# Small VectorE operations issued in a row, sixteen steps of attention read out in float32, and another block order in the last step

## The chip, the cores and the metric

The kernel runs on one core of a Trainium2 chip. Its engines are TensorE (PE; PEld is its weight load), VectorE (DVE), ScalarE (ACT), GpSimd (POOL) and SyncE (SP, which here issues nearly all DMAs). The metric is device time in microseconds (us): the median of three runs, 929.9 us (929.48 to 930.02). Times in rows count from the start of the profiled span.

## The reference

Attention with a memory, then two feed-forward layers ("MoE"), each with two matrix products:

```python
# B, H, S, D = 4, 8, 576, 64; 2304 tokens, d_model 512, d_ff 2048
scores = where(causal, -1e9, q @ k.T / sqrt(D)); a = softmax(scores); local = a @ v
q_p = where(q > 0, q, exp(q) - 1) + 1
mem_out = (q_p @ M_prev) / (q_p @ z_prev + 1e-6)
x = g * mem_out + (1 - g) * local                 # g = sigmoid(beta) per head
h = x @ moe_w_in;  x = (h * sigmoid(h)) @ moe_w_out
h = x @ moe2_w_in; return (h * tanh(softplus(h))) @ moe2_w_out
```

## The kernel before

**Attention** works on pairs of heads. A visit is one pair and either its first two blocks of 128 queries or its last three; the 16 visits of the first kind come first. A step is one block of queries of a visit (`STEPS`), in three stages. `stage_a`: scores (PE), their maximum (DVE, L613), the exponential (ACT), and P, the unnormalized weights, brought into transposed form. `stage_b`, three steps later: P times V and the memory product (PE), then, at a visit's last step, a chain of DVE operations: the denominators (add, reciprocal, multiply: 8 columns each) and the scaled result (512 columns). `stage_c`: a transpose and the way to `xs0` or DRAM.

P is transposed in two ways. In the first `TURNED` = 8 steps PE transposes the float32 P, ACT copies it out of PSUM, and P times V is one float32 matmul per block of keys. In later steps ACT and DVE split P into two float16 parts (`copy`, `stt`), a DMA transposes them, and each block of keys takes three float16 matmuls; V is then split too (`prep_v`: a DVE maximum at L538, a PE sum, three small DVE operations, ACT, DVE).

**Weights** of the first MoE come in 16 units of 1 MB, 0 to 7 for `w_in` and 8 to 15 for `w_out`. Each is rebuilt from 64-bit words (`single`: two ACT operations, one DVE), and PE multiplies it with itself (a gram matrix; `banks<-w 128x128` in the rows) for a bound of its size. `part_scale` turns the bound into a scale by a chain of small DVE operations (`largest`, `inverse`), for `w_in` in two halves and for `w_out` once; then ACT and DVE split each unit into two float16 parts (`weight_split`; `w<-w,wsc` in the rows).

**The MoE** runs in 9 chunks of 256 tokens, 8 units of width each. `chunk_x` loads and scales a chunk's inputs (`xh<-xs,xsc`); `gemm1` (`banks<-xh,w`), `hidden` and `gemm2` (`banks<-g,w`) follow. The second MoE is alike, with 7 products in place of 8 (`p` in `gemm2`); `flush2` combines the 7 blocks on ACT and DVE and stores them.

**The order** of all this is set by `Plan`: every operation is recorded with its reads, writes and priority, and `issue` walks through modelled time, giving each engine the ready operation with the lowest priority number. The engines then run their lists in that order, and an instruction whose input is late holds all behind it. When PE is idle in the plan between 18 and 75 us, it gets filler matmuls (`L474`).

Of the kernel before, what the change touches and what calls it, by code (L numbers as in the profile page):

```python
# [9 lines left out]
F32 = mybir.dt.float32  # L10
# [37 lines left out]
TURNED = 8  # L48
FILL_FROM, FILL_TO, FILL_PART, FILL_NS = 18e3, 75e3, 0.6, 28
PARTS = 2  # L50
# [12 lines left out]
class Plan:  # L63
# [6 lines left out]
    def __init__(self):  # L70
        self.ops, self.seen, self.shared, self.fill = [], {}, set(), None
# [13 lines left out]
    def add(self, prio, choices, writes, reads, tail=0, edge=(0, 0, (False, False), (False, False)), shared=False):  # L85


        k, deps = len(self.ops), set()
        for regs, w in ((reads, False), (writes, True)):
            for r in [y for x in regs for y in self.regions(x)]:  # L90
                log = self.seen.setdefault(r[0], [])
                keep = []
                for e in log:
                    _, a0, a1, b0, b1, op, ew = e
                    hit = a0 < r[2] and r[1] < a1 and b0 < r[4] and r[3] < b1
                    if hit and (w or ew) and op != k:
# [100 lines left out]
def attn_moe_moe2_kernel(ctx: ExitStack, tc: tile.TileContext, kq, vm, beta, w1, w2, out):  # L197
# [13 lines left out]
    plan = Plan()  # L211
# [285 lines left out]
    def load_vm(v, prio):  # L497
        p, _, nk = VISITS[v]
        n = nk * 2 * (D + 1)
        if 2 * v < TURNED:  # L500
            t = phs[v // 2 * 2].rearrange("p n c -> p (n c)").bitcast(F32)[:, 260 * (v % 2):260 * (v % 2) + n]
        else:
            t = rvr()[:, 0:n]
        rm[v] = rmr()
        rv[v] = t.rearrange("p (n e d) -> p n e d", n=nk, e=2)
        dma(prio, t, vm[p, :, 130:130 + n], reads=[])
        dma(prio, rm[v], vm[p, :, 0:130], reads=[])
# [22 lines left out]
    def prep_v(v, prio):  # L530
# [10 lines left out]
        mm(prio, [(total, ones, top, True, True)])  # L541
        ts(prio, inv[:, 0:2], total.to_broadcast([128, 2]), 2.0**-14, ALU.mult, 1e-30, ALU.max)
        ts(prio, inv[:, 0:2].bitcast(U32), inv[:, 0:2].bitcast(U32), 0x7F800000, ALU.bitwise_and)
        other(prio, "DVE", 80, lambda: nc.vector.reciprocal(out=scale, in_=inv[:, 0:1]), [scale], [inv])
        plan.add(prio, [c_act(v1[:, :, :, 0:D], x, AF.Copy, scale), (*c_ts(v1[:, :, :, 0:D], x, scale, ALU.mult), VC)],
# [97 lines left out]
    def stage_b(n, prio):  # L643
# [37 lines left out]
        each = lambda y: y.unsqueeze(1).to_broadcast([128, m, 4])  # L681
        tt(prio, den, g[:, :, :, D], each(eps[:, 4 * (n < TURNED):4 * (n < TURNED) + 4]), ALU.add)
        other(prio, "DVE", 90, lambda: nc.vector.reciprocal(out=den, in_=den), [den], [den])
        tt(prio, den, den, each(gvv), ALU.mult)
        tt(prio, t4, g[:, :, :, 0:D], den.unsqueeze(3).to_broadcast([128, m, 4, D]), ALU.mult)
        tt(prio, x, t4[:, :, 0:2], t4[:, :, 2:4], ALU.add, ("POOL", "DVE"))
# [29 lines left out]
    def largest(prio, s, top, spot, root=0.0):  # L716


        d, m = diagr(), mxr()[:, 1:2]
        if cols(top) == 128:  # L720
            stt(prio, d, top, 1e-30, ident, ALU.max, ALU.mult)
        else:
            ts(prio, d, ident, top, ALU.mult, 1e-30, ALU.max)
        if spot is None:
            o = banks[:, 512 * 6:512 * 8].rearrange("p (b c) -> p b c", b=2)[:, :, 388:452]
            mm(prio, [(o[:, i], onesf, d[:, 64 * i:64 * i + 64], True, True) for i in range(2)])
            reduce(prio, m, o, ALU.max, mybir.AxisListType.XY)
# [15 lines left out]
    def part_scale(g, prio):  # L743

        c, w = cvec[0], wsc[0]
        if g < PARTS:
            largest(prio, w[:, g:g + 1], gram[0], bank[0], WMAX[0][0] / 4)
            inverse(prio, c[:, 4 + g:5 + g], w[:, g:g + 1])
            ts(prio, c[:, 4 + g:5 + g], c[:, 4 + g:5 + g], 0.5, ALU.mult)
            return  # L750
# [6 lines left out]
        ts(prio, c[:, 2:3], t, 0.5, ALU.mult)  # L757

    def weight_scale(l, k, prio, spot):
# [10 lines left out]
        else:  # L770
            tt(prio, c[:, 2:3], c[:, 2:3], p, ALU.mult)

# [80 lines left out]
    def chunk_x(l, c, prio, spot):  # L853
# [7 lines left out]
        top = top[:, 0:1]  # L861
        reduce(prio, top, r, ALU.max, mybir.AxisListType.XY, True)
        tt(prio, t16, top, top, ALU.mult)
        mm(prio, [(spot, ones, t16, True, True)])
        ts(prio, p, spot, 1e-36, ALU.max)
        inverse(prio, s, p)
        ts(prio, s.bitcast(U32), s.bitcast(U32), 1, ALU.logical_shift_right, 0x7F800000, ALU.bitwise_and)
        ts(prio, s, s, 2.0**64 * XNORM, ALU.mult)
        if l == 0:
# [11 lines left out]
        inverse(prio, p, s)  # L881
# [68 lines left out]
    def gemm2(l, j, g, yo, prio):  # L950
        if l == 1:
            for p in (2, 1, 4, 6, 7, 5, 3):
# [91 lines left out]
    def weights_of(k, gate=()):  # L1044

        nonlocal n_att
        for u in range(NU // 2 * k, NU // 2 * (k + 1)):
# [5 lines left out]
            if k == 0 and j == NU // 2 // PARTS - 1:  # L1053
                part_scale(g, w_prio(u))
                for w in range(u - j, u + 1):
                    weight_split(w, w_prio(u))
        if k == 1:
            part_scale(PARTS, w_prio(u))
# [55 lines left out]
    for i, (l, c, j) in enumerate(steps):  # L1114
# [7 lines left out]
        gemm2(l, j, g_of.pop(i), y_of[l, c], 1e6 + i)  # L1122
# [55 lines left out]
```

## Time and profile before

| | |
|---|---|
| median of three runs | 929.9 us |
| the profiled execution, its span | 929.32 us, 927.3 us |
| busy PE, DVE, ACT, POOL | 897.8, 706.9, 594.7, 438.5 us |
| granted TensorE clock, mean of the span | 0.997 |

Busy time is the union of an engine's instructions, so a wait between two of them is not in it. In a timeline row the first number is the start, the second the time from the first start to the last end of what is merged in the row ("x8"), and in brackets stands the idle time before it with what ended it.

### The profile page before, as it was taken

Reading aid. Unit: us, or ns where it says so; the run is one execution under the profiler, and the core shown is the slowest. Engines: PE = TensorE matmul, PEld = TensorE weight load, DVE = VectorE, ACT = ScalarE, POOL = GpSimd, SP = SyncE. Lnnn points to the kernel's source line nnn. Section 1 sums busy time; section 2 is a strip of 40 time slices with the busy share of each in tenths; the row PEclk is TensorE's granted clock in tenths of the full one; section 3 lists DMA queues with packets and bytes.
Section 4 is the critical chain, followed back from the end, with each engine's and each line's share of the span. In section 5 each row is a group of like instructions: output and inputs, shape, how many; then the busy total and the mean of one; then the engine's idle time right before and its main releaser. Section 6 shows DMA issues by size and latency. Waiting matters only on the chain.

```text
span 927.3 us, 26260 instructions
## 1 busy us (share of the span) xinstructions
PE 897.8 (97%) x10830; PEld 808.4 (87%) x10830; DVE 706.9 (76%) x1512; ACT 594.7 (64%) x1032; POOL 438.5 (47%) x653
## 2 busy tenths in 40 slices
PE   6889799999999999999999999999999999999997
PEld 5778688888888888888988889999999999999996
DVE  4798977887988688878567465578787887887775
ACT  6799878788687787866465445445455545644553
POOL 3104223645555444564477466363554644635443
PEclk9999999999999999999999999999999999999999
DMA  8799589898999898985434353301010010010010
GB/s 272 260 226 290 161 185 312 204 272 215 240 249 239 241 226 208 231 179 102 115 116 126 136 172 126 104 25 47 19 31 25 25 47 25 24 47 17 10 24 23
DMA packets 148759, 129.77 MB, mean 140 GB/s; under 512 B 105376, under 2 KB 132512, under 8 KB 144544
## 3 DMA queue, kind: packets, MB, share of 16 engines
q1 hardware_dynamic: 148496, 128.10, 52.0%
q8 instruction: 84, 1.38, 0.6%
q14 instruction: 35, 0.29, 0.1%
q10 hardware_dynamic: 144, 0.00, 0.0%
HBM read 77.75 MB, written 25.69 MB: 112 GB/s over the span
## 4 chain that ended last, share of the span: by engine, by line
PE 91%; ACT 4%; DVE 3%; issue 1%; SPq 0%; DMA 0%; DVEq 0%; ACTq 0%
PE banks L427 89%; ACT arena L359 2%; PE banks L435 1%; DVE w L367 1%; ACT w L779 1%; DVE arena L373 1%; ACT w L359 1%; DVE arena L613 0%; PE banks L474 0%; SPq L441 0%; ACT ws L359 0%; DMA arena<-vm 0%; DVE arena L367 0%; DVE ws L367 0%; ACT ga L359 0%
## 5 line engine op out<-in xcount | busy, mean ns | idle before, releaser
L427 PEld LDWEIGHTS <-w 128*128 128x128 f16 (+1 forms) x3584 | 342.0, 98 | 41.1 <-issue 2.1
L427 PE MATMUL banks<-arena 128*128 128x128 f16 (+5 forms) x4728 | 287.2, 221 | 5.8 <-ACT arena L359 4.6
L427 PEld LDWEIGHTS <-arena 128*128 128x128 f16 x4392 | 226.0, 98 | 7.5 <-issue 4.4
L427 PE MATMUL banks<-xh,w 128*128 128x256 f16 x1728 | 206.6, 273 | 0.0
L427 PE MATMUL banks<-g,w 128*128 128x256 f16 x1728 | 205.5, 273 | 0.0
L373 POOL TENSOR_TENSOR arena<-arena 128x4 f32<-128x4 f32 (+3 forms) x147 | 96.8, 663 | 178.6 <-DVE arena L373 78.8
L427 PE MATMUL banks<-w,g 128*128 128x256 f16 x1512 | 178.9, 273 | 0.0
L427 PEld LDWEIGHTS <-g 128*128 128x128 f16 x1512 | 144.4, 98 | 15.2
L373 POOL TENSOR_TENSOR g<-ga,g 128x512 f16<-128x512 f32 x72 | 96.3, 1340 | 69.3 <-ACT g L359 68.9
L359 ACT ACTIVATE arena<-arena 128x256 f32<-128x256 f32 (+7 forms) x169 | 98.9, 606 | 32.7 <-PE banks L427 30.5
L373 POOL TENSOR_TENSOR w<-w 128x128 f32<-128x128 f32 x138 | 78.3, 590 | 87.1 <-ACT w L359 85.5
L367 DVE SCALAR_TENSOR_TENSOR arena<-arena 128x640 f16<-128x640 f32 (+6 forms) x132 | 105.5, 805 | 12.6 <-ACT arena L359 9.6
L373 POOL TENSOR_TENSOR xh<-xh 128x128 f32<-128x128 f32 x138 | 68.2, 516 | 53.7 <-ACT xh L359 51.9
L359 ACT ACTIVATE arena<-banks,arena 128x128 f32<-128x128 f32 (+4 forms) x144 | 74.5, 551 | 21.0 <-DVE arena L613 16.2
L359 ACT ACTIVATE ga<-banks,xsc 128x512 f32<-128x512 f32 x72 | 49.4, 686 | 48.6 <-PE banks L427 46.5
L367 DVE SCALAR_TENSOR_TENSOR g<-w,xsc,g 128x384 f16<-128x384 f32 (+1 forms) x72 | 52.1, 725 | 29.2 <-ACT g L359 29.2
L613 DVE TENSOR_REDUCE arena<-banks 128x2 f32<-128x256 f32 (+3 forms) x80 | 63.6, 802 | 13.8 <-PE banks L427 11.8
L367 DVE SCALAR_TENSOR_TENSOR ga<-ga,banks 128x512 f32<-128x512 f32 x72 | 48.8, 680 | 31.9 <-ACT ga L359 31.6
L359 ACT ACTIVATE w<-banks 128x128 f32<-128x128 f32 x72 | 19.7, 273 | 62.4 <-PE banks L427 62.3
L373 DVE TENSOR_TENSOR arena<-banks,arena 128x8 f32<-128x8 f32 (+1 forms) x96 | 36.3, 378 | 29.4 <-PE banks L427 14.7
L367 DVE SCALAR_TENSOR_TENSOR g<-xh,xsc,g 128x384 f16<-128x384 f32 (+1 forms) x72 | 53.5, 746 | 5.9 <-ACT g L359 4.5
L359 ACT ACTIVATE g<-w,xsc 128x384 f16<-128x384 f32 (+1 forms) x72 | 47.4, 661 | 10.6 <-POOL w L373 10.0
(128 smaller groups left out, 1142.8 us busy)
## 6 DMA issues: line engine op xcount, KB each, us to landing
ws<-w SPq DMA_DIRECT2D x22, 1024.0 KB, 7.0
arena<-kq SPq DMA_DIRECT2D x16, 576.0 KB, 4.8
w<-w SPq DMA_DIRECT2D x8, 1024.0 KB, 5.6
wd<-w SPq DMA_DIRECT2D x16, 512.0 KB, 3.7
arena<-vm SPq DMA_DIRECT2D x16, 325.0 KB, 4.2
yd<-w SPq DMA_DIRECT2D x36, 128.0 KB, 2.7
ws<-wd SPq DMA_DIRECT2D x9, 512.0 KB, 4.3
xs<-yd SPq DMA_DIRECT2D x9, 512.0 KB, 3.7
```

The source lines that it names most:

```text
L359: return ("ACT", ns, lambda: nc.scalar.activation(out=out, in_=in_, func=func, scale=scale, bias=bias))
L367: return ("DVE", 1.04 * cols(out) + 160 - over[0], lambda: nc.vector.scalar_tensor_tensor(out=out, in0=in0, scalar=s, in1=in1, op0=op0, op ...
L373: return (e, ns, lambda: eng.tensor_tensor(out=out, in0=in0, in1=in1, op=op))
L427: nc.tensor.matmul(out=o, lhsT=l, rhs=r, start=a, stop=z)
L435: plan.add(prio, [("PE", 109, lambda: nc.tensor.transpose(o, x, ident))], [o], [x, ident], edge=(107, 109, (False, False), (False, False)))
L613: other(prio, "DVE", 1.04 * cols(both) + 70, lambda: nc.vector.tensor_reduce(out=m1, in_=both, axis=AX, op=ALU.max, negate=True), [m1], [b ...
L779: plan.add(prio, [("ACT", 0.833 * 1024 + 115, lambda: nc.scalar.activation(out=w, in_=high.bitcast(F32), func=AF.Prelu, scale=2.0**-112, a ...
```

## The change

Four things change. (1) `Plan` can record several small DVE operations as one (`begin`, `close`): they are then issued one behind the other, with nothing between. This is done for the denominators with the scaled result, the three small operations of `prep_v`, the chains of `part_scale` and `weight_scale`, and two in `chunk_x`, whose `inverse(p, s)` moves up. (2) `TURNED` is 16, so visits 4 to 7 take the float32 way too; all eight visits keep V in `phs`, three to a buffer. (3) `part_scale` gets priority -3e5 (before: `w_prio`, about -2e5 for `w_in` and 35 for `w_out`). (4) The last `gemm2` takes its blocks in the order 1, 7, 2, 6, 4, 5, 3.

```diff
-TURNED = 8
+TURNED = 16
...
+    def begin(self):
+        self.run = []
+
+    def close(self, prio):
+        run, self.run = self.run, None
+        cs = [next(c for c in r[0] if c[0] == "DVE") for r in run]
+        def go():
+            for c in cs:
+                c[2]()
+        return self.add(prio, [("DVE", sum(c[1] for c in cs), go)], [x for r in run for x in r[1]],
+                        [x for r in run for x in r[2]], shared=any(r[3] for r in run))
...
         if 2 * v < TURNED:
-            t = phs[v // 2 * 2].rearrange("p n c -> p (n c)").bitcast(F32)[:, 260 * (v % 2):260 * (v % 2) + n]
+            t = phs[v // 3].rearrange("p n c -> p (n c)").bitcast(F32)[:, 260 * (v % 3):260 * (v % 3) + n]
...
+        plan.begin()
         tt(prio, den, g[:, :, :, D], each(eps[:, 4 * (n < TURNED):4 * (n < TURNED) + 4]), ALU.add)
         other(prio, "DVE", 90, lambda: nc.vector.reciprocal(out=den, in_=den), [den], [den])
         tt(prio, den, den, each(gvv), ALU.mult)
         tt(prio, t4, g[:, :, :, 0:D], den.unsqueeze(3).to_broadcast([128, m, 4, D]), ALU.mult)
+        plan.close(prio)
...
+        plan.begin()
         ts(prio, p, spot, 1e-36, ALU.max)
         inverse(prio, s, p)
         ts(prio, s.bitcast(U32), s.bitcast(U32), 1, ALU.logical_shift_right, 0x7F800000, ALU.bitwise_and)
         ts(prio, s, s, 2.0**64 * XNORM, ALU.mult)
+        inverse(prio, p, s)
+        plan.close(prio)
...
-            for p in (2, 1, 4, 6, 7, 5, 3):
+            for p in (1, 7, 2, 6, 4, 5, 3) if ended else (2, 1, 4, 6, 7, 5, 3):
...
-            part_scale(PARTS, w_prio(u))
+            part_scale(PARTS, -3e5)
```

The instructions move as follows. First VectorE, where the scale of `w_out` is made; `mx_84` is the bound, `wsc_0_89` the scales, `cvec_0_91` the constants made of them, and `arena_95` belongs to attention. Before:

```order
L376 TENSOR_REDUCE mx_84<-banks 128x1
L367 SCALAR_TENSOR_TENSOR arena_95<-arena_95 128x256
L741 RECIPROCAL wsc_0_89<-mx_84 128x1
L367 SCALAR_TENSOR_TENSOR arena_95<-arena_95 128x256
L364 TENSOR_SCALAR wsc_0_89<-wsc_0_89 128x1
L367 SCALAR_TENSOR_TENSOR arena_95<-arena_95 128x512
L364 TENSOR_SCALAR wsc_0_89<-wsc_0_89 128x1
L373 TENSOR_TENSOR arena_95<-banks,arena_95 128x8
L364 TENSOR_SCALAR arena_95<-arena_95 128x2
L613 TENSOR_REDUCE arena_95<-banks 128x2
L373 TENSOR_TENSOR cvec_0_91<-cvec_0_91,wsc_0_89 128x1
L683 RECIPROCAL arena_95<-arena_95 128x8
```

With the change:

```order
L394 TENSOR_REDUCE mx_84<-banks 128x1
L765 RECIPROCAL wsc_0_89<-mx_84 128x1
L382 TENSOR_SCALAR wsc_0_89<-wsc_0_89 128x1 x2
L394 TENSOR_REDUCE cvec_0_91<-wsc_0_89 128x1
L391 TENSOR_TENSOR cvec_0_91<-cvec_0_91,wsc_0_89 128x1
L385 SCALAR_TENSOR_TENSOR wsc_0_89<-cvec_0_91 128x2
L765 RECIPROCAL cvec_0_91<-cvec_0_91 128x1
L382 TENSOR_SCALAR cvec_0_91<-cvec_0_91 128x1
L385 SCALAR_TENSOR_TENSOR ga_78<-ga_78,banks 128x512
L391 TENSOR_TENSOR xsc_86<-cvec_0_91,xsc_86 128x1
L385 SCALAR_TENSOR_TENSOR arena_95<-arena_95 128x256
L385 SCALAR_TENSOR_TENSOR w_72<-w_72,wsc_0_89 128x1024
```

Before, eight operations of the chain took up 20 places of the list, with twelve of attention between them (the last is `L364` on `cvec_0_91`, eight rows further down; a ninth came earlier). Now the nine stand together (`x2` is two of them).

Next, VectorE at the start of the program. L538 (L556 after the change) is the maximum of V in `prep_v`, L613 (L633) that of the scores. Before:

```order
L538 TENSOR_REDUCE arena_95<-arena_95 128x1
L613 TENSOR_REDUCE arena_95<-banks 128x2 x2
L538 TENSOR_REDUCE arena_95<-arena_95 128x1
L613 TENSOR_REDUCE arena_95<-banks 128x2 x2
L364 TENSOR_SCALAR arena_95<-banks 128x2
L364 TENSOR_SCALAR arena_95<-arena_95 128x2
L544 RECIPROCAL arena_95<-arena_95 128x1
L364 TENSOR_SCALAR arena_95<-arena_95 128x4x64
```

With the change:

```order
L633 TENSOR_REDUCE arena_95<-banks 128x2 x4
L556 TENSOR_REDUCE arena_95<-arena_95 128x1 x2
L391 TENSOR_TENSOR arena_95<-banks,arena_95 128x8
L704 RECIPROCAL arena_95<-arena_95 128x8
L391 TENSOR_TENSOR arena_95<-arena_95 128x8
L391 TENSOR_TENSOR arena_95<-banks,arena_95 128x512
L385 SCALAR_TENSOR_TENSOR w_72<-w_72,ws_76 128x1024
L633 TENSOR_REDUCE arena_95<-banks 128x2 x2
```

The maximum of V, of the first visit that takes the float16 way, stood ahead of the scores' and now stands behind them, and the first chain of denominators has moved ahead of the first rebuilt unit (`w_72<-w_72,ws_76`).

Last, SP at the start of the program: `vm` is V and the memory matrices, `kq` keys and queries, `w` the weight units. Before:

```order
L441 DMA arena_95<-vm 128x260 x3
L441 DMA arena_95<-vm 128x130
L441 DMA arena_95<-vm 128x260
L441 DMA ws_76<-w 128x2048
L441 DMA ws_77<-w 128x2048
L441 DMA g_75<-w 128x2048
L441 DMA arena_95<-kq 128x2x256 x2
L441 DMA arena_95<-vm 128x260
```

With the change:

```order
L459 DMA arena_95<-vm 128x260 x3
L459 DMA arena_95<-vm 128x130
L459 DMA arena_95<-vm 128x260 x5
L459 DMA arena_95<-kq 128x2x256
L459 DMA ws_76<-w 128x2048
L459 DMA ws_77<-w 128x2048
L459 DMA g_75<-w 128x2048
L459 DMA arena_95<-kq 128x2x256
```

Four more loads of V and one of keys and queries now stand ahead of the first three weight units.

## Rows read from the trace of the kernel before

**Rows 1.** Busy time by stretch; the bracket counts instructions, PEclk is the granted clock
```profile
0.00:61.50 61.50, 47.40 (x671) 40.58 (x672) 40.97 (x100) 45.78 (x81) 13.78 (x37) 1.00 0.79 261
61.50:94.90 33.40, 31.83 (x355) 27.54 (x354) 29.79 (x54) 31.92 (x60) 13.01 (x10) 1.00 1.06 264
94.90:103.60 8.70, 3.68 (x40) 2.98 (x40) 8.21 (x28) 5.74 (x12) 1.72 (x3) 0.91 0.74 203
103.60:150.00 46.40, 44.62 (x466) 37.85 (x465) 39.55 (x99) 37.12 (x79) 11.46 (x15) 0.98 0.79 191
150.00:450.00 300.00, 298.95 (x3464) 259.55 (x3462) 245.22 (x475) 230.79 (x393) 147.63 (x203) 1.00 0.91 219
450.00:920.60 470.60, 470.60 (x5837) 439.56 (x5835) 340.26 (x754) 242.91 (x411) 250.85 (x387) 1.00 0.19 60
```
Columns: stretch and length, then PE, PEld, DVE, ACT, POOL, PEclk, DMA share, GB/s.

**Rows 2.** Timeline of PE, 94 to 105 us
```profile
94.26 0.62 PE L427 MATMUL banks<-w 128*128 128x128 bf16 x8
...
96.06 0.49 PE L427 MATMUL banks<-diag,onesf 128*128 128x128 f32 x2 [1.18 <-DVE diag L367]
...
102.26 0.16 PE L427 MATMUL banks<-arena,ones 128*128 128x1 bf16 x1 [3.86 <-DVE arena L538]
...
103.58 1.49 PE L427 MATMUL banks<-g,w 128*128 128x256 f16 x6
```

**Rows 3.** Timeline of DVE in the chain of the scale of w_out
```profile
96.60 0.28 DVE L376 TENSOR_REDUCE mx<-banks 128x1 f32<-128x128 f32 x1
...
97.13 0.15 DVE L741 RECIPROCAL wsc<-mx 128x1 f32<-128x1 f32 x1
97.20 0.40 DVE L367 SCALAR_TENSOR_TENSOR arena<-arena 128x256 f32<-128x256 f32 x1
...
100.20 0.15 DVE L367 SCALAR_TENSOR_TENSOR wsc<-cvec 128x2 f32<-128x2 f32 x1
```

**Rows 4.** Timeline of ACT, the first split units of w_out
```profile
101.29 2.18 ACT L359 ACTIVATE w<-w,wsc 128x1024 f16<-128x1024 f32 x2
```

**Rows 5.** Timeline of DVE, two dependent small operations with nothing between
```profile
10.84 0.17 DVE L364 TENSOR_SCALAR arena<-arena 128x2 uint32<-128x2 uint32 x1
11.05 0.16 DVE L544 RECIPROCAL arena<-arena 128x1 f32<-128x1 f32 x1
```

**Rows 6.** Timeline of PE: P times V in float32, transposes, P times V in float16
```profile
33.45 1.38 PE L427 MATMUL banks<-arena 128*128 128x65 f32 x10 [0.47 <-ACT xs L359]
34.66 0.82 PE L435 MATMUL banks<-ident,arena 128*128 128x128 f32 x6
...
71.52 0.83 PE L427 MATMUL banks<-arena 128*128 128x65 f16 x14
```

**Rows 7.** ACT by form, 58.9 to 101.3 us (busy us, mean ns of one)
```profile
L359 ACT ACTIVATE arena<-arena 128x256 f16<-128x256 f32 x7 | 3.0, 449 | 0.0
...
L359 ACT ACTIVATE arena<-arena 128x512 f16<-128x512 f32 x4 | 2.5, 625 | 0.0
```

**Rows 8.** DVE by form, 58.9 to 101.3 us
```profile
L367 DVE SCALAR_TENSOR_TENSOR arena<-arena 128x256 f16<-128x256 f32 x6 | 4.1, 686 | 0.0
...
L367 DVE SCALAR_TENSOR_TENSOR arena<-arena 128x512 f16<-128x512 f32 x4 | 3.6, 890 | 0.1
```

**Rows 9.** Timeline of SP, DVE and ACT at the program's start
```profile
2.13 4.39 SPq L441 DMA_DIRECT2D arena<-vm  x9
...
7.95 0.42 DVE L538 TENSOR_REDUCE arena<-arena 128x1 bf16<-128x256 f32 x1 [1.34 <-DMA arena<-vm]
...
9.39 0.37 ACT L359 ACTIVATE arena<-banks,arena 128x128 f32<-128x128 f32 x1 [3.37 <-DVE arena L613]
```

**Rows 10.** Timeline of PE, ACT and DVE at the end
```profile
918.83 2.46 PE L427 MATMUL banks<-w,g 128*128 128x256 f16 x21
...
920.66 0.47 ACT L359 ACTIVATE w<-banks,xsc 128x256 f32<-128x256 f32 x1 [2.43 <-PE banks L427]
...
921.17 0.75 DVE L367 SCALAR_TENSOR_TENSOR ws<-banks,xsc,w 128x512 f32<-128x512 f32 x1 [2.15 <-ACT w L359]
```

More of the change, by code (lines that the diff above doesn't have):

```diff
@@ L70, in __init__ @@
     def __init__(self):
-        self.ops, self.seen, self.shared, self.fill = [], {}, set(), None
+        self.ops, self.seen, self.shared, self.fill, self.run = [], {}, set(), None, None
     @staticmethod
@@ L85, in add @@
     def add(self, prio, choices, writes, reads, tail=0, edge=(0, 0, (False, False), (False, False)), shared=False):
+        if self.run is not None:
+            self.run.append((choices, writes, reads, shared))
+            return
         k, deps = len(self.ops), set()
@@ L726, in largest @@
             mm(prio, [(o[:, i], onesf, d[:, 64 * i:64 * i + 64], True, True) for i in range(2)])
+            plan.begin()
             reduce(prio, m, o, ALU.max, mybir.AxisListType.XY)
@@ L730, in largest @@
             mm(prio, [(o, onesf, d, True, True)])
+            plan.begin()
             reduce(prio, m, o, ALU.max, AX)
@@ L749, in part_scale @@
             ts(prio, c[:, 4 + g:5 + g], c[:, 4 + g:5 + g], 0.5, ALU.mult)
+            plan.close(prio)
             return
@@ L757, in part_scale @@
         ts(prio, c[:, 2:3], t, 0.5, ALU.mult)
+        plan.close(prio)
     def weight_scale(l, k, prio, spot):
@@ L771, in weight_scale @@
             tt(prio, c[:, 2:3], c[:, 2:3], p, ALU.mult)
+        plan.close(prio)
     def single(r, w, prio):
@@ L861, in chunk_x @@
         top = top[:, 0:1]
+        plan.begin()
         reduce(prio, top, r, ALU.max, mybir.AxisListType.XY, True)
         tt(prio, t16, top, top, ALU.mult)
+        plan.close(prio)
         mm(prio, [(spot, ones, t16, True, True)])
+        plan.begin()
         ts(prio, p, spot, 1e-36, ALU.max)
@@ L868, in chunk_x @@
         ts(prio, s, s, 2.0**64 * XNORM, ALU.mult)
+        inverse(prio, p, s)
+        plan.close(prio)
         if l == 0:
@@ L880, in chunk_x @@
                 stt(prio, lo, v, s, hi, ALU.mult, ALU.subtract)
-        inverse(prio, p, s)
         if l == 0:
@@ L948, in hidden2, with gemm2 @@
         return g
-    def gemm2(l, j, g, yo, prio):
+    def gemm2(l, j, g, yo, prio, ended=False):
         if l == 1:
-            for p in (2, 1, 4, 6, 7, 5, 3):
+            for p in (1, 7, 2, 6, 4, 5, 3) if ended else (2, 1, 4, 6, 7, 5, 3):
                 a, b, o = ORDER_A[p], ORDER_B[p], yo[p]
@@ L1053, in weights_of @@
             if k == 0 and j == NU // 2 // PARTS - 1:
-                part_scale(g, w_prio(u))
+                part_scale(g, -3e5)
                 for w in range(u - j, u + 1):
@@ L1121, in attn_moe_moe2_kernel @@
             tt(MOE, sc[:, 2:3], cvec[0][:, 2:3], sc[:, 3:4], ALU.mult)
-        gemm2(l, j, g_of.pop(i), y_of[l, c], 1e6 + i)
+        gemm2(l, j, g_of.pop(i), y_of[l, c], 1e6 + i, i == len(steps) - 1)
         if (l, c, j) == (0, NT // TOK - 1, NF // 2 - 2):
```

## Prediction

> **What bounds the kernel now.** I read busy time by stretch first, since a share over the whole span mixes stages with different limits. From 150 us to the last matmul PE is busy for 298.95 of 300.00 and 470.60 of 470.60 us [rows 1]: there it is the bound, and nothing that VectorE (DVE) or ScalarE (ACT) saves shows in the time. PE stands still earlier. Until 61.5 us it waits for weights, scores and scales (47.40 us busy, much of it filler). From 61.5 to 94.9 us it runs the first gemm1 with attention and weight bounds between, 31.83 of 33.40 us. From 94.9 to 103.6 us it is busy for 3.68 of 8.70 us, with the granted clock at 0.91 on average [rows 1]. The timeline says why: the last bound of a weight unit ends at 94.88, the matmul that spreads it starts at 96.06, and the first gemm2 only at 103.58 [rows 2]. Between lie the scale's chain on DVE, whose maximum starts at 96.60 and whose last link that the splits need starts at 100.20 [rows 3], and the split on ACT at 101.29 [rows 4]. A link takes 0.15 us; what makes 3.6 us of it is other work between the links. So the time is the moment of the first gemm2 plus a stretch that PE fills, plus the tail. I work out how that moment moves.
>
> **Extra PE work.** Four visits change over. In float32, P times V of a visit's second step takes 1.38 us (10 records), in float16 0.83 us (14 records) [rows 6]. By record that is 0.138 and 0.059 us, so the first steps take 6 x 0.138 = 0.83 against 8 x 0.059 = 0.47 us. Six transposes take 0.82 us [rows 6]. A visit costs 0.55 + 0.36 + 0.82 = 1.7 us more, four cost 6.9 us. Where that lies decides what it costs: by the order of instructions, 14 of the 24 new transposes stand ahead of the first gemm1 matmul, where PE has room, and 10 between it and the first gemm2. In that second part float32 P times V costs 16 x 2 records x 0.138 = 4.4 us where float16 took 74 x 0.059 = 4.4 us, because fewer steps stand there; six or so float16 records (0.5 us) and ten transposes (1.4 us) come on top, eight more bound matmuls 0.6 us (0.62 for eight [rows 2]), and filler (17 matmuls) and one visit's scores go, some 1.5 us. Net +1.0 us.
>
> [...]
>
> **What ACT and DVE lose before w_out can be split.** Between the first scaling of x and the first split of w_out the order shows 70 ACT instructions before and 60 after: nine fewer of 256 columns and three fewer of 512 from P's and V's float16 parts, three more of 256 and two more of 512 for reading out PSUM, two of 512 of the MoE and, net, one of 1024 gone to another place. At 0.449 and 0.625 us [rows 7] and 1.09 us (2.18 for two [rows 4]): -6 x 0.449 - 3 x 0.625 - 1.09 = -5.7 us; neighbours overlap by some 0.1 us, so I take -5. DVE has 81 and 58 there: six of 256 and three of 512 go, 6 x 0.686 + 3 x 0.890 = 6.8 us [rows 8], and smaller ones, some 2.5 us.
>
> **What a row of small operations costs.** Two dependent small operations with nothing between start 0.21 us apart [rows 5]; with other work between, the small one takes 0.07 us of the engine (97.13 to 97.20 [rows 3]). So each link inside a row costs DVE about 0.13 us in which it does nothing. In this part 17 links do so: 2.2 us, which leaves DVE 7 us less. For the chain itself the sum is the other way: seven links of 0.21, 1.5 us, from the maximum's start to the end of what the splits need, in place of 100.35 - 96.60 = 3.75 us: -2.3 us. Bounds: 0 if the split on ACT is held by its queue anyway, -4.0 if ACT takes it at once (101.29 - 96.60 less 0.7). On this the skill ("VectorE: DVE Perf Modes", The DRAIN you can't avoid) would differ: the flush between two operations comes with a semaphore or without. By it rows would cost DVE nothing, and the rivals below that live from links would have no price; the two starts above disagree with that.
>
> **The start.** Until the first scaling of x, ACT has 80 instructions before and 83 after, with sums that agree within 0.5 us; DVE has 99 and 106, 3.2 us more, mostly two split units that are drawn ahead, and 38 links in rows, 4.9 us. Against that, DVE is busy only 40.97 of 61.50 us there, ACT 45.78 [rows 1], and one wait goes: the first exponentials start at 9.39, held by a V maximum that waits for its load until 7.95 [rows 9], and this now stands behind the scores' maxima; the scores' maximum could start some 1.3 us earlier. Against it again, five more loads ahead of the first weights cost SP 5 x 4.39 / 9 = 2.4 us [rows 9]. I take zero for the start, between -5 (the 1.3 us and a quarter of ACT's 15.7 idle us) and +8.1 (DVE's additions with no idle time given back).
>
> **The sum.** PE, from 61.5: 31.83 + 3.68 + 1.0 gives 98.0 us. The splits: 101.29 - 5 - 2.3 = 94.0, and 2.3 us from split to gemm2 as before, 96.3 us. PE is the later one, so the first gemm2 starts at 98.0 in place of 103.58: -5.6 us. The halt of 3.86 us [rows 2] shrinks, and with it the slow clock behind it: 9% of 8.70 and 2% of 46.4 us [rows 1], 1.7 us, between 0 and that; I take 1.5. In the tail, ACT starts at 920.66, when the block pair (1, 7), fifth in the old order, is done: PE starts that group at 918.83 and takes three matmuls of 0.109 us a block, 918.83 + 5 x 0.327 = 920.47 and 0.2 to be seen [rows 10]. In the new order the pair is done after two blocks, and DVE's first operation waits for the fourth instead: 918.83 + 1.31 + 0.2 = 920.34 in place of 921.17 [rows 10], -0.8 us; its five operations then follow unchanged. Block 7 needs the later half of g, so this could shrink to 0. Everything else runs beside a full PE. Sum: -5.6 - 1.5 - 0.8 = -7.9 us. The profiled execution took 929.32 us, 0.6 below the median; from the median, 929.9 - 7.9 = 922.0 us.
>
> **Rivals.**
> The start gets shorter. For it speaks the idle time of ACT and DVE above; against it the 8.1 us that DVE gets. At the bound, -5: 917 us. 12%.
> The start gets longer and eats the gain. DVE carries +8.1 us and gives no idle time back: gemm1 starts at 69.6, gemm2 at 69.6 + 36.5 = 106.1, +2.5; the clock saves nothing, the tail 0.8: 931.6 us at the full price, 929 to 930 at three quarters. Against it: DVE's idle 20 us there. 12%, most of it no change.
> Rows starve the MoE (slower). From 150 to 450 us DVE is busy 245.22 of 300 us [rows 1], and the order holds 16 rows of `prep_v`, 33 of denominators and 5 pairs in `chunk_x`: 156 links, 20 us at 0.13. DVE then stands at 88% on average, and where attention for the next chunk comes late, PE waits. The point: over 7.9 us of PE waits in that stretch, where now there are 1.05. At the full 20 us 942 us, at half to two thirds 932 to 935; I take 934. For it: DVE holds its queue in order. Against it: 35 us stay free, and PE shows no wait now. 13%.
> The change does nothing there: the moment of gemm2 is set by the arrival of weights, not by ACT and DVE. Then only the tail shows, 929.1 us. Against it: ACT is busy 31.92 of 33.40 us before that moment [rows 1]. 4%.
>
> **The numbers.** Forecast 59%, 922.0 us with its own range 918 to 927. A measurement of this kernel can tell about 0.2%, 1.9 us, from no change. Faster: forecast, the shorter start and a part of the longer, 0.77. Same: 0.09. Slower: 0.14. The range from 915.5 to 930.5 leaves out the starved MoE and the far end of the shorter start.
>
> **What would show it.** Right: the first `banks<-g,w` matmul at 96 to 100 us; nine DVE operations in some 1.9 us before it; no slow clock near 100 us; PE full from there, with under 2 us of waits between 150 and 450; the first `flush2` operation on ACT 1 us before PE ends. Wrong: gemm1 starting after 65 us, or gaps of PE between 150 and 450 us with DVE as what ends them.

## The result, and the profile after

The kernel after takes 943.23 us (median of five, 940.34 to 945.11), the kernel before 929.9 (929.48 to 931.23): 1.0139 times as long, 95% interval 1.0127 to 1.0151. The forecast was 922.0. The profiled execution after took 945.11 us with a span of 943.3, against 927.3 before.

Busy time by stretch in the kernel after, to be held against [rows 1]. The columns are the same; the cuts are at the first gemm1 matmul (71.95), the first gemm2 matmul (108.2) and PE's last matmul:

```profile
0.00:61.50 61.50, 47.77 (x497) 39.80 (x498) 38.13 (x85) 39.77 (x75) 9.45 (x35) 0.94 0.73 245
61.50:71.95 10.45, 9.98 (x144) 9.34 (x144) 8.28 (x22) 6.86 (x10) 0.95 (x1) 0.72 0.58 208
71.95:108.20 36.25, 34.73 (x350) 30.08 (x346) 31.73 (x59) 32.32 (x60) 12.47 (x9) 1.00 0.66 226
108.20:150.00 41.80, 39.64 (x418) 33.99 (x419) 36.39 (x75) 34.59 (x71) 8.65 (x9) 1.00 0.61 150
150.00:450.00 300.00, 292.58 (x3320) 251.60 (x3317) 248.10 (x458) 229.03 (x394) 147.65 (x195) 1.00 0.88 219
450.00:937.66 487.66, 484.84 (x6034) 450.92 (x6032) 355.38 (x794) 256.96 (x426) 268.05 (x388) 1.00 0.20 62
```

Three things stand there. gemm1 begins at 71.95 us where it began at 61.62. From gemm1 to gemm2 it takes 36.25 us in place of 41.96. And from 150 to 450 us PE stands still for 7.42 us where it stood for 1.05, with 2.82 us more behind that, where there was nothing. The span's 16.0 us are then: the start +10.3, gemm1 to gemm2 -5.7, PE's idle time from gemm2 on +9.6 (2.16 + 7.42 + 2.82 against 1.78 + 1.05), PE's busy time from gemm2 on +2.2 (39.64 + 292.58 + 484.84 = 817.06, against 814.87 with the last matmul's end at 921.28), the tail -0.4.

The stretch between the two gemms took what was forecast (36.25 us, forecast 36.5). PE's timeline there, answering to [rows 2]; behind the matmul that spreads the bounds, gemm1 now fills what was a halt of 3.86 us:

```profile
101.69 0.62 PE L445 MATMUL banks<-w 128*128 128x128 bf16 x8
...
103.99 0.39 PE L445 MATMUL banks<-diag,onesf 128*128 128x128 f32 x2
...
104.43 3.11 PE L445 MATMUL banks<-xh,w 128*128 128x256 f16 x27
...
108.22 0.28 PE L445 MATMUL banks<-g,w 128*128 128x256 f16 x1 [0.19 <-ACT w L377]
```

The scale's chain on DVE, answering to [rows 3]: one row, with 1.15 us from the maximum to the start of the link that gives the split its scale, where there were 3.60 us.

```profile
104.80 0.28 DVE L394 TENSOR_REDUCE mx<-banks 128x1 f32<-128x128 f32 x1
105.12 0.16 DVE L765 RECIPROCAL wsc<-mx 128x1 f32<-128x1 f32 x1
105.32 0.34 DVE L382 TENSOR_SCALAR wsc<-wsc 128x1 uint32<-128x1 uint32 x2
105.58 0.14 DVE L394 TENSOR_REDUCE cvec<-wsc 128x1 f32<-128x2 f32 x1
105.75 0.16 DVE L391 TENSOR_TENSOR cvec<-cvec,wsc 128x1 f32<-128x1 f32 x1
105.95 0.16 DVE L385 SCALAR_TENSOR_TENSOR wsc<-cvec 128x2 f32<-128x2 f32 x1
```

ACT's first split of w_out follows at 106.99, 2.19 us behind the maximum's start; before it was 4.69 us [rows 3, 4].

```profile
106.99 1.17 ACT L377 ACTIVATE w<-w,wsc 128x1024 f16<-128x1024 f32 x1
```

The start is another matter. PE's timeline there shows the clock: ten float32 matmuls of P times V take 2.35 us at 24.86, 1.28 us at 31.58 and, behind a run of short gaps, 2.49 us at 38.70. The bounds of the second half of w_in reach their spreading matmul only at 63.78 (54.65 before).

```profile
24.86 2.35 PE L445 MATMUL banks<-arena 128*128 128x65 f32 x10
...
31.58 1.28 PE L445 MATMUL banks<-arena 128*128 128x65 f32 x10
33.70 0.44 PE L453 MATMUL banks<-ident,arena 128*128 128x128 f32 x2 [0.84 <-ACT arena L377]
...
34.98 0.44 PE L453 MATMUL banks<-ident,arena 128*128 128x128 f32 x2 [0.62 <-ACT arena L377]
...
38.70 2.49 PE L445 MATMUL banks<-arena 128*128 128x65 f32 x10
...
58.66 0.63 PE L445 MATMUL banks<-w 128*128 128x128 bf16 x8 [1.95 <-DVE w L385]
...
63.78 0.77 PE L445 MATMUL banks<-diag,onesf 128*128 128x128 f32 x2
```

In the kernel after the granted clock is 0.50 (1.2 GHz of 2.4) from 36.57 to 43.40 and from 60.47 to 67.29:

```profile
36.57:43.40 6.83, 6.83 (x43) 5.79 (x41) 3.32 (x10) 3.50 (x6) 0.68 (x3) 0.50 0.45 144
60.47:67.29 6.82, 5.33 (x46) 5.07 (x46) 5.22 (x15) 2.99 (x7) 0.95 (x1) 0.50 0.83 310
```

In the kernel before it is 0.50 once, near 100 us:

```profile
101.98:105.40 3.42, 3.14 (x21) 2.27 (x22) 3.39 (x7) 3.42 (x7) 0.48 (x1) 0.50 0.73 174
```

Work that PE does at half speed takes twice its time (2.49 against 1.28 us above), so the slow clock costs PE at most half of 6.83 + 5.33 us, 6.1, against 1.6 us before. The 1.00 that the pages print for the first 27 to 30 us is no measurement in most traces: these hold no record of the clock there, as the 2.35 us at 24.86 show.

What PE waits for in the middle is best seen at one place. DVE and PE of the kernel after, around 247 us:

```profile
245.36 0.49 PE L445 MATMUL banks<-xh,w 128*128 128x256 f16 x3
...
246.21 0.15 DVE L391 TENSOR_TENSOR arena<-banks,arena 128x4 f32<-128x4 f32 x1
246.39 0.18 DVE L704 RECIPROCAL arena<-arena 128x4 f32<-128x4 f32 x1
...
246.60 0.16 DVE L391 TENSOR_TENSOR arena<-arena 128x4 f32<-128x4 f32 x1
246.87 0.42 DVE L391 TENSOR_TENSOR arena<-banks,arena 128x256 f32<-128x256 f32 x1
...
247.35 0.18 PE L445 MATMUL banks<-arena,ones 128*128 128x1 bf16 x1 [1.50 <-DVE arena L391]
...
247.39 0.49 PE L445 MATMUL banks<-xh,w 128*128 128x256 f16 x3
```

A row of four denominator operations ends at 247.29; the small matmul, which writes into a PSUM bank that the row reads, waits 1.50 us for it, and the gemm1 matmuls that stand behind it in PE's order start 0.04 us after it. No single wait is long. By releaser, from 110 to 600 us of the kernel after (us in total, times, longest):

```profile
PE banks L445 <- DVE arena L391: 4.6, 7, 1.5
PE banks L445 <- ACT arena L377: 3.6, 6, 1.3
PE banks L445 <- DVE ga L385: 2.1, 2, 1.2
```

All seven waits of the first line (4.6 us) end 0.05 to 0.14 us after the last operation of a row of denominators.

The tail moved by one block: from the start of ACT's first operation to PE's end it is 0.95 us (937.66 - 936.71), before 0.62 (921.28 - 920.66).

```profile
932.80 4.86 PE L445 MATMUL banks<-w,g 128*128 128x256 f16 x43
```

```profile
936.71 0.47 ACT L377 ACTIVATE w<-banks,xsc 128x256 f32<-128x256 f32 x1 [2.09 <-PE banks L445]
```

### The profile page after: what moved, and what is told of

It reads as the page before. It is cut to its first block, busy times and chain, and to the rows that moved or that the text cites. A ratio compares the mean times of both kernels' runs of the same rounds, so it can differ in the third digit from the quotient of the medians.

```text
span 943.3 us, 26020 instructions
## 1 busy us (share of the span) xinstructions
PE 909.5 (96%) x10749; PEld 815.7 (86%) x10749; DVE 720.4 (76%) x1492; ACT 599.5 (64%) x1032; POOL 447.2 (47%) x637
## 4 chain that ended last, share of the span: by engine, by line
PE 85%; DVE 9%; ACT 2%; issue 1%; DMA 1%; POOL 0%; DVEq 0%; ACTq 0%; SPq 0%
PE banks L445 83%; DVE w L385 2%; DVE arena L385 2%; DVE arena L391 2%; PE banks L453 1%; ACT arena L377 1%; DMA ws<-w 1%; DVE arena L633 1%; DVE ga L385 1%; DVE xh L385 1%; PE banks L492 0%; DVE arena L704 0%; DMA arena<-kq 0%; ACT w L377 0%; DVE mx L394 0%
## 5 line engine op out<-in xcount | busy, mean ns | idle before, releaser
L445 PE MATMUL banks<-arena 128*128 128x128 f16 (+6 forms) x4704 | 292.2, 223 | 6.7 <-ACT arena L377 5.3
L445 PEld LDWEIGHTS <-arena 128*128 128x128 f16 x4320 | 222.8, 98 | 6.1 <-issue 3.1
L391 POOL TENSOR_TENSOR arena<-arena 128x256 f32<-128x256 f32 (+3 forms) x145 | 106.5, 743 | 162.2 <-DVE arena L391 116.7
L391 POOL TENSOR_TENSOR w<-w 128x128 f32<-128x128 f32 x143 | 81.9, 593 | 94.6 <-ACT w L377 92.9
L385 DVE SCALAR_TENSOR_TENSOR arena<-arena 128x640 f16<-128x640 f32 (+6 forms) x120 | 101.8, 866 | 7.9 <-ACT arena L377 4.9
L377 ACT ACTIVATE arena<-arena 128x256 f32<-128x256 f32 (+6 forms) x162 | 96.2, 617 | 14.1 <-PE banks L445 5.7
L391 POOL TENSOR_TENSOR xh<-xh 128x128 f32<-128x128 f32 x133 | 72.6, 566 | 60.2 <-ACT xh L377 58.6
L377 ACT ACTIVATE arena<-banks,arena 128x128 f32<-128x128 f32 (+4 forms) x144 | 73.8, 551 | 29.5 <-DVE arena L633 21.3
L633 DVE TENSOR_REDUCE arena<-banks 128x2 f32<-128x256 f32 (+3 forms) x80 | 63.2, 805 | 17.8 <-PE banks L445 17.3
L377 ACT ACTIVATE g<-ga 128x512 f16<-128x512 f32 x70 | 43.9, 629 | 22.9 <-DVE ga L385 22.8
```

Source lines behind the costliest of these rows:

```text
L377: return ("ACT", ns, lambda: nc.scalar.activation(out=out, in_=in_, func=func, scale=scale, bias=bias))
L385: return ("DVE", 1.04 * cols(out) + 160 - over[0], lambda: nc.vector.scalar_tensor_tensor(out=out, in0=in0, scalar=s, in1=in1, op0=op0, op ...
L391: return (e, ns, lambda: eng.tensor_tensor(out=out, in0=in0, in1=in1, op=op))
L445: nc.tensor.matmul(out=o, lhsT=l, rhs=r, start=a, stop=z)
L633: other(prio, "DVE", 1.04 * cols(both) + 70, lambda: nc.vector.tensor_reduce(out=m1, in_=both, axis=AX, op=ALU.max, negate=True), [m1], [b ...
```

## The experiments

All were timed in alternation with the kernel before (930.3 to 930.8 us beside them). The moments are of each run's profiled execution; "PE idle" is PE's idle time from 150 to 600 us, and "half clock" the time from 33 us to PE's last matmul in which the granted clock is 0.50.

| run | us | ratio to before, 95% | first gemm1 | first gemm2 | PE idle, us | half clock, us |
|---|---|---|---|---|---|---|
| before | 929.9 | | 61.6 | 103.6 | 1.1 | 3.4 |
| after | 943.2 | 1.0127 to 1.0151 | 72.0 | 108.2 | 10.2 | 13.7 |
| 1 rows alone | 949.2 | 1.0178 to 1.0217 | 66.8 | 111.4 | 9.9 | 13.7 |
| 2 sixteen alone | 932.7 | 1.0001 to 1.0026 | 69.6 | 108.2 | 1.5 | 10.2 |
| 3 after, eight steps | 949.8 | 1.0187 to 1.0219 | 62.8 | 109.4 | 9.6 | 20.5 |
| 4 after, no rows | 929.3 | 0.9973 to 1.0006 | 66.9 | 109.5 | 2.5 | 0 |
| 5 rows, denominators | 948.8 | 1.0179 to 1.0212 | 66.6 | 117.1 | 6.6 | 23.9 |
| 6 rows, values | 929.5 | 0.9977 to 0.9996 | 63.1 | 103.9 | 0.8 | 10.2 |
| 7 rows, scales | 930.6 | 0.9996 to 1.0016 | 60.6 | 100.9 | 4.7 | 3.4 |
| 8 all rows, links at 0.13 | 935.1 | 1.0040 to 1.0070 | 64.2 | 107.6 | 2.7 | 6.8 |
| 9 denominators, links at 0.13 | 937.3 | 1.0053 to 1.0083 | 62.8 | 109.8 | 3.4 | 10.2 |
| 10 scratch, not counted | 933.9 | 1.0024 to 1.0044 | 62.7 | 104.6 | 1.6 | 6.8 |
| 11 scratch, counted | 936.7 | 1.0045 to 1.0086 | 62.3 | 109.7 | 3.3 | 6.8 |
| 12 values, order, priority | 932.3 | 1.0006 to 1.0025 | 61.3 | 104.3 | 3.0 | 6.8 |
| 13 rows in the old order | 937.7 | 1.0067 to 1.0098 | 64.2 | 108.7 | 2.7 | 10.2 |
| 14 rows not marked | 964.9 | 1.0353 to 1.0387 | 65.1 | 114.5 | 19.6 | 23.9 |
| 15 links at 0.22 | 940.5 | 1.0097 to 1.0127 | 61.4 | 110.8 | 6.0 | 17.1 |
| 16 V loads late | 927.7 | 0.9959 to 0.9979 | 63.8 | 102.9 | 2.7 | 0 |
| 17 as 13, own gates | 938.6 | 1.0069 to 1.0097 | 63.6 | 109.4 | 3.6 | 10.2 |
| 18 as 16, and 6 | 927.7 | 0.9956 to 0.9980 | 62.5 | 102.2 | 4.5 | 0 |

**Which part costs (runs 1 to 4).** The change was cut into rows (`begin`, `close` and the moved reciprocal of `chunk_x`) and the rest. Runs 1 and 2 put one part on the kernel before; runs 3 and 4 take one part from the kernel after.

```
 run 2, on before:    -TURNED = 8            +TURNED = 16
                      ... phs[v // 2 * 2] ...  becomes  ... phs[v // 3] ...
 run 3, on after:     the same lines the other way
 run 4, on after:     -plan.begin()          -plan.close(prio)
```

> The kernel before with the rows of small VectorE operations alone (same block order, same sixteen-less attention, same priorities). Before 929.9, after 943.2 us. Theory R (the rows cost: DVE does nothing between the links and the attention of the next chunk comes late): nearly the whole loss is here, 938 to 943 us, PE waits between 150 and 450 us of 5 us or more. Theory L (the load queue and the start: the float32 steps push weights behind V loads): no loss here, 929 to 931 us, PE waits under 2 us there. If both share it: 933 to 937.

> The kernel before with sixteen float32 attention steps alone. Theory L: the first gemm1 starts at 68 us or later (61.6 before) since the first weights are issued behind five more loads, and the time is 936 to 942 us. Theory R: the start is moved by 2 us at most, the time stays at 928 to 931 us or falls, since ACT and DVE have less to do.

> The kernel after with eight float32 steps again: rows, block order and the priority of the scales stay. Theory R: the loss stays, 938 to 943 us. Theory L: it goes, 928 to 931 us, with the first gemm1 near 62 us.

> The kernel after with the small VectorE operations placed singly again, as in the kernel before; sixteen float32 steps, block order and the priority of the scales stay. Theory R: 922 to 931 us, PE waits between 150 and 450 us under 2 us. Theory L: the loss at the start stays, 936 to 943 us, first gemm1 at 68 us or later.

The rows are the loss, as theory R said, though runs 1 and 3 lie 6 us and more above its range: alone they cost 18.7 us, and the kernel after without them is level with the kernel before. The sixteen steps alone cost 2.2 us, less than theory L and more than theory R allowed, and move gemm1 by 8.0 us, as theory L had it, but little of that reaches the end. Among rows they even give back 6.5 us (run 3 against after). In the two traces PE's idle time falls by 5.7 us (33.8 against 39.5) and the half clock from 20.5 to 13.7 us; why was not tried. Run 4 also shows that the moment of the first gemm2 does not fix the time: it lies at 109.5, 5.9 us later than before, and the time is the same. PE has been busy for 92.6 us by then in place of 82.9, and no half clock shows.

**Which rows (runs 5 to 7).** Rows at one kind of place only, on the kernel before.

```
 run 5: begin/close in stage_b alone
 run 6: begin/close in prep_v alone
 run 7: begin/close in largest, part_scale, weight_scale, chunk_x alone
```

> The kernel before with rows for the denominators alone (4 operations each, 48 rows). All rows together cost 18.7 us. Theory I (idle links: each costs DVE 0.13 us, and the time lost goes with the number of links): the denominators hold about two thirds of all links, so two thirds of the loss, 941 to 944 us, PE waits of 5 us or more between 150 and 600 us. Theory S (the loss comes from the rows of the weights' and x's scales, at the start): 930 to 932 us.

> The kernel before with rows for the scale of the values alone (3 operations each, 28 rows, 12 of them ahead of 104 us). Theory I: a fifth of the links, 933 to 935 us. Theory S: 930 to 932 us.

> The kernel before with rows for the scales of the weights and of x alone (3 row ends for the first layer's weights, 2 for the second's, 2 rows a chunk). Theory I: a tenth or so of the links, 930 to 933 us. Theory S: the first gemm2 comes 5 us or more later than 103.6 us, 936 us or more.

The denominators alone bring the whole loss, 18.4 us; the values' rows gain a little and those of the scales change nothing. Theory I, by which the loss goes with the number of links, had two thirds for the denominators and a fifth for the values: it fails on both. Theory S fails too: the scales' rows move the first gemm2 forward by 2.7 us, not back by 5.

Where run 5 loses its time is more than the waits from 150 us on. Over its whole profiled span PE is idle for 36.7 us (946.9 - 910.2) where it was 29.5 (927.3 - 897.8), 7.2 us more. And the granted clock is 0.50 in two stretches, in which PE works for 6.29 + 13.31 us where it worked 3.14 before:

```profile
55.31:62.14 6.83, 6.29 (x68) 5.50 (x69) 5.59 (x12) 5.89 (x13) 0.20 (x1) 0.50 0.81 232
103.10:120.17 17.07, 13.31 (x92) 10.26 (x93) 13.88 (x36) 11.81 (x23) 3.06 (x3) 0.50 0.73 189
```

Half of that is 9.8 us against 1.6, up to 8.2 us more. Waits and slow clock together make up to 15.4 of the 19.6 us by which the span grew, and the slow clock may well be the larger part.

**Is it time on DVE that the planner does not know of (runs 8 to 11)?** The planner counts a row as the sum of its operations, and each link as nothing; an operation placed singly is taken to start 0.22 us after the end of the one that it needs. Runs 8 and 9 count the links. Run 10 has no rows: every instruction of every engine stands in its old order, and three scratch reciprocals, each needing the last, follow each denominators' reciprocal unseen by the planner. Run 11 lets it count them.

```
 runs 8, 9: -... ("DVE", sum(c[1] for c in cs), go) ...
            +... ("DVE", sum(c[1] for c in cs) + 130 * (len(cs) - 1), go) ...
 run 10:    -other(prio, "DVE", 90, lambda: nc.vector.reciprocal(out=den, in_=den), ...)
            +def slow():
            +    nc.vector.reciprocal(out=den, in_=den)
            +    for i in range(3):
            +        nc.vector.reciprocal(out=spare[:, (i + 1) % 2:(i + 1) % 2 + 1], in_=spare[:, i % 2:i % 2 + 1])
            +other(prio, "DVE", 90, slow, [den], [den])
 run 11:    +other(prio, "DVE", 560, slow, [den], [den])
```

> All rows on the kernel before, as in the run with the rows alone, but the planner counts 0.13 us for each link inside a row, which it took for nothing. Theory I: the links still cost what they cost, 943 to 949 us. Theory P (the planner believes DVE free too early and places what follows in a bad order): most of the loss goes, 930 to 936 us.

> Rows for the denominators alone, with each link counted by the planner at 0.13 us. Unpriced, these rows alone took 948.8 us. Theory P (VectorE time that the planner does not know of makes the loss: every engine's order is then wrong for what runs): 931 to 936 us, PE waits under 3 us between 110 and 600 us. Theory W (a row waits with everything behind it until all its inputs are there, and holds VectorE's queue): pricing links changes nothing of that, 943 us or more.

> The kernel before, without any row and with every other instruction in its old order; behind each of the 48 reciprocals of denominators VectorE runs three operations on a scratch column that each need the last (some 0.4 to 0.5 us together), and the planner does not know of them. The output is unchanged by them. Theory P: the loss of the rows comes back without rows, 942 to 955 us, PE waits of 6 us or more between 110 and 600 us. Theory W: 930 to 935 us, since nothing waits as a block and VectorE has 35 us free of 300.

> The same three scratch operations beside each reciprocal, but counted by the planner at 0.47 us. Theory P: VectorE has the time if the orders are made for it, 931 to 936 us. If VectorE's time itself is the bound there, planned or not: 940 us or more.

Counting the links takes 14.1 of 18.7 us from all rows and 11.5 of 18.4 from the denominators, in theory P's range for run 8 and 1.3 us above it for run 9. But run 10 refutes P as it was put: the unseen time alone costs 3.1 us (933.9 against 930.8), which theory W had. Theory W fails on run 9. Run 11 fits neither of its two forecasts: a planner that knows of the scratch time ends at 936.7 us, 2.9 us later than one that doesn't. That the time was really added shows on DVE's timeline of run 10, where the three scratch operations hold the engine from 203.95 to 204.39; over the 48 places they hold it for 0.41 to 0.45 us each, 20.6 us together.

```profile
202.53 0.16 DVE L374 TENSOR_TENSOR arena<-banks,arena 128x4 f32<-128x4 f32 x1 [0.35 <-ACT arena L360]
...
203.86 0.17 DVE L686 RECIPROCAL arena<-arena 128x4 f32<-128x4 f32 x1
203.95 0.52 DVE L688 RECIPROCAL spare<-spare 128x1 f32<-128x1 f32 x3
204.39 0.14 DVE L365 TENSOR_SCALAR arena<-banks 128x2 f32<-128x2 f32 x1
...
206.69 0.15 DVE L374 TENSOR_TENSOR arena<-arena 128x4 f32<-128x4 f32 x1
...
207.50 0.41 DVE L374 TENSOR_TENSOR arena<-banks,arena 128x256 f32<-128x256 f32 x1
```

**The row or the order (runs 13 and 17).** The kernel before is planned as before, and only when its instructions are written the first three operations of each denominator are held back and set in a row with the fourth, at the fourth's place. All other engines keep their order, which the traces of runs 10 and 17 bear out: PE's 10830 instructions stand in the same order as before. In run 13 the third operation so reads, in places, a gate that a later visit has already replaced; run 17 gives each gate a place of its own.

```
...
+for i, (c, w, r, s) in enumerate(row):
+    plan.add(prio, [(c[0], c[1], lambda i=i: put(i))], w, r, shared=s)
 put(i) keeps operation i; put(3) issues all four
 ...
 run 17: +gates = ring(carve([4], F32, 16))
```

> Rows of denominators without a new plan: the kernel before, planned as before, with the orders of TensorE, ScalarE, GpSimd and the queues unchanged to the last instruction; on VectorE the first three operations of each denominator are only held back and issued in a row with the fourth, at the fourth's old place. Theory B (a row as such, its links and the block it makes in VectorE's queue, costs the time): 942 us or more. Theory O (the rows are cheap, and what costs is the order that the planner makes of all engines once it takes each row for one piece with links of no length): 930 to 935 us, like the scratch operations.

> As the run with rows of denominators in the old order, but each gate has a place of its own for 16 visits (the run before let the held-back third operation read gates that a later visit had already replaced in places); TensorE, ScalarE, GpSimd and the queues keep the order of the kernel before to the last instruction. If those replaced gates had no part in the time: 936 to 939 us, so that a row as such costs 6 to 8 us and the planner's new order the other 10 or so of the 18. If they had: near 934 us, as with the scratch operations.

The same denominator as above, on DVE's timeline of run 17:

```profile
209.56 0.15 DVE L374 TENSOR_TENSOR arena<-banks,arena 128x4 f32<-128x4 f32 x1
209.74 0.18 DVE L686 RECIPROCAL arena<-arena 128x4 f32<-128x4 f32 x1
209.96 0.16 DVE L374 TENSOR_TENSOR arena<-arena 128x4 f32<-128x4 f32 x1
210.22 0.42 DVE L374 TENSOR_TENSOR arena<-banks,arena 128x256 f32<-128x256 f32 x1
```

Starts lie 0.18, 0.22 and 0.26 us apart, 0.66 us in all, where three slots of 0.07 stood [rows 3]: 0.45 us a denominator, as much as the scratch operations take. A row as such costs 8.0 us (938.6 against 930.5); theory B asked for 942 or more, theory O for 935 or less, and the truth lies between. The same time on DVE costs 3.1 us when it stands beside the denominators and 8.0 us when it stands right in front of the fourth operation, which lets go of the PSUM banks; that this is why was not tried apart. The other 10.3 of the 18.4 us are the order that the planner makes for rows with links of no length.

**What leads the planner there (runs 14 and 15).**

```
 run 14: -... [x for r in run for x in r[2]], shared=any(r[3] for r in run))
         +... [x for r in run for x in r[2]])
 run 15: +... ("DVE", sum(c[1] for c in cs) + 220 * (len(cs) - 1), go) ...
```

> Rows of denominators alone, links still counted at nothing, but a row no longer marked as one that shares a port with GpSimd (of its four operations only the third carries the mark when placed singly, and the row carries it as a whole, so that the planner puts the row behind GpSimd's work). Unmarked, theory M (the mark makes the bad order): 930 to 938 us. Theory O by the links' length alone: 945 to 950 us, unchanged.

> Rows of denominators alone, with each link counted at 0.22 us, the length that the planner gives a step from one VectorE operation to the next that needs it when they are placed singly. At 0: 948.8 us, at 0.13: 937.3 us. Theory O by the links' length: 930 to 937 us, at or below the time for 0.13. If the plans merely scatter: anywhere from 932 to 949, with no order in the three numbers.

Without the mark the time is 964.9 us: no theory had that. Theory M has its sign wrong: with the mark the time is 16 us shorter. By the length that the planner gives a link, the times stand at 948.8 (0), 937.3 (0.13) and 940.5 us (0.22): a row with links of no length is the worst, and the other two lie about the 938.6 of rows in the old order. Between 0.13 and 0.22 no trend can be told, and run 15 lies above the 937 that theory O allowed; plans scatter by a few us (runs 6, 7 and 12 lie between 929.5 and 932.3). That the 964.9 belong to the same line, because the planner then also leaves out the wait for the port, is a reading and not shown.

**A better version (runs 12, 16 and 18).**

```
 run 12, on before: prep_v's rows, the block order, part_scale(..., -3e5)
 run 16, on run 4:  -load_vm(v + 1, att_prio(n, L_V) - 1e6)
                    +load_vm(v + 1, att_prio(n, L_V) - 1e6 if v < 3 else -1.9e5)
 run 18, on run 16: prep_v's rows
```

> A version meant to beat both: the kernel before with rows for the scale of the values alone, the new block order of the last step and the new priority of the weights' scales. The values' rows alone gave 929.5, the order takes 0.3 us from the tail as the trace after has it, the priority is open: 927 to 930 us. If the priority shortens the stretch before the first gemm2 as the prediction had it (5 us): 923 to 926.

> The kernel after without rows (929.3 us, first gemm1 at 66.9 us), with the V loads of the fourth and later visits behind the first layer's w_in weights in priority, so that only four visits' loads stand ahead of the first weights in the sync queue, as in the kernel before. Theory L (sixteen float32 steps make the start longer through this queue): the first gemm1 at 62 to 65 us and the time 925 to 928 us. If the start is longer by the work itself: first gemm1 at 66 to 68, time 928 to 931 us.

> The best version so far (927.7 us: sixteen float32 steps, new block order and priority, no rows, later V loads behind the weights) with rows for the scale of the values added, which took 1.0 us from the kernel before. If the two add up: 926 to 927.5 us. If the values' rows gained by the scatter of plans alone: 926 to 931 us, and no better than without them.

Run 12 missed: the priority does not shorten the stretch ahead of gemm2 (104.3), and with 932.3 us it is slower than run 6, which has less in it. Run 16 bears out theory L in time and in gemm1. Run 4, which differs from it in the loads alone, issues the first weights behind 13 `vm` loads, where nine stood before [rows 9], and the first two units of the second half of w_in at 23.17 and 28.64:

```profile
2.13 6.29 SPq L441 DMA_DIRECT2D arena<-vm  x13
...
9.21 1.07 SPq L441 DMA_DIRECT2D ws<-w  x2
...
23.17 0.59 SPq L441 DMA_DIRECT2D w<-w  x1
...
28.64 0.42 SPq L441 DMA_DIRECT2D w<-w  x1
```

In run 16 seven stand ahead, and those two units go at 18.71:

```profile
2.13 3.44 SPq L441 DMA_DIRECT2D arena<-vm  x7
5.62 0.90 SPq L441 DMA_DIRECT2D ws<-w  x2
...
18.71 0.90 SPq L441 DMA_DIRECT2D w<-w  x2
```

The last two units go at much the same time in both (33.69 and 40.06 in run 4, 34.11 and 39.59 in run 16), so it is the early ones that gain: DVE rebuilds the third unit at 19.79 in place of 29.47. gemm1 begins 3.1 us earlier than in run 4, and the 927.7 us beat both kernels (0.9969 of before, 0.9959 to 0.9979). The values' rows add nothing to that, so their 1.0 us in run 6 does not carry over; the scatter of plans would explain it.

## Why the prediction was wrong

**Right, by their mechanism and nearly their size.** The row of the scale's chain: -2.5 us from maximum to split (4.69 to 2.19), forecast -2.3. The slow clock near 100 us is gone (granted 1.00 from 71.95 on). The cost of a link, 0.13 us [rows 3, 5]: the row in run 17 shows 0.45 us for three. The four visits' 6.9 us of PE work: run 4 has 4.8 us more PE busy time than before and lacks the slow clock near 100 us, which had cost 1.6, so 6.4.

**Right in size, and partly by luck.** The stretch from gemm1 to gemm2 took 36.3 us, forecast 98.0 - 61.5 = 36.5. The forecast had PE busy in all of it, with 1.0 us more work than before; PE was busy for 34.73 us (35.37 before) and idle for 1.5. How much of the 5.7 us is due to the shorter chain and the work that ACT and DVE lose was not tried apart. gemm1 began 10.3 us later, which left more time for the work ahead of w_out's split, and the stretch is 38.6 us in run 2, with sixteen steps and no rows, but 42.5 in run 4.

**The tail's term was mis-sized.** -0.8 was forecast; -0.33 us came, one block of three matmuls, and the end of the span against PE's end moved by 0.4 (5.64 against 6.0). The forecast let ACT start behind the second block and DVE behind the fourth. The trace has ACT start 0.95 us before PE's end, with three blocks of 0.327 us still to come, so behind the fourth, and DVE 0.5 us later; what held ACT until then stays open.

**"I take zero for the start" failed.** It grew by 10.3 us, past the bound of 8.1. The bound was made of DVE's additions; the runs show other things. The five loads put off the first weights by 2.6 us (9.13 against 6.57), near the 2.4 that the text names, but the sum has nothing for it; moving the V loads back is worth 3.1 us at gemm1 and 1.6 us at the end (run 16 against 4). And PE works for 12.2 us at half speed in two stretches of the start, up to 6.1 us, where the sum took 1.5 us of slow clock away. Sixteen steps alone move gemm1 by 8.0 us, rows alone by 5.2 (runs 2 and 1). How the 10.3 us divide among these stays open.

**The rival that starves the MoE came true, and was held for too unlikely and priced by the wrong thing.** Its place and sign were right: waits of 7.4 us from 150 to 450. In the sum this stood as "Everything else runs beside a full PE", a term of nothing; from gemm2 on PE's idle time grew by 9.6 us. It was given 13%, with "35 us stay free" against it. That argument was about DVE's time, and on DVE's time it is nearly right: 20.6 us more of it cost 3.1 us (run 10). What the prediction did not do was to ask what a row does to the orders. `close` hands the planner one piece without its links, where single operations carried 0.22 us each; all engines are then ordered for denominators that are done sooner than they can be, and PE, which works its order off strictly, waits at each place where they are not. From the order of instructions the prediction took counts, and not what stands behind a row in PE's queue. That the length which the planner gives a row sets some 10 us is shown by runs 5, 9, 15 and 17; that it acts through the small matmuls behind rows, as at 247.35 us, is read from traces and not tried apart, and in run 5 the slow clock ahead of and behind gemm2's start takes up to as much as the waits.

**The frame was too narrow as well.** "The moment of the first gemm2 plus a stretch that PE fills" misled twice: run 4 has it 5.9 us later at no loss. What adds up is PE's idle time, its slow clock and its work over the whole span: from before to after +4.3 us (943.3 - 909.5 against 927.3 - 897.8), +4.5 (half of 12.2 against half of 3.1) and 7.2 that are left over. These should be the extra work, forecast at 6.9, but they are a remainder and no measurement.

Open: why sixteen float32 steps give back 6.5 us among rows, and what lets the clock fall. That gaps of PE as such do it is not shown: from 30 us to gemm1 PE was idle for 6.27 of 31.62 us in the kernel before, at a granted clock of 1.00, and for 7.28 of 41.95 us in the kernel after, at 0.84.

## What to carry to other kernels

Where a planner orders engines that work their queues strictly in order, a piece that is glued together must carry its length; a few tenths of a us too little, at 48 places, cost some 10 us, while 20.6 us of work that nobody planned for cost 3. The true length does not make glue free: 6.5 to 10 us stayed (runs 9, 15 and 17). Glue only what is on the critical chain and rare (the scale's chain: -2.5 us there), and not what frees a PSUM bank on every visit. And count what a new early load stands in front of in its queue, not just its own issue.

## What the hardware showed that was not expected

Idle time on an engine that is 82% busy is a better cushion than thought: some 0.43 us added 48 times to DVE, with nothing reordered, moved the end by 3.1 us. And PE's slow clock can weigh as much as its waits. In the kernel after the granted clock fell to 0.50 at 36.57 us, behind waits of 0.84 and 0.62 us with filler between, and ten matmuls took 2.49 in place of 1.28 us; in run 5 it stood at 0.50 for 17.07 us around the first gemm2, up to 6.7 us of its loss.
